# Late weight loads on ScalarE's queue, the last normalisation on VectorE, and the result's check behind the last product

## The chip, the cores and the metric

The kernel runs on one core of a Trainium2 chip. The metric is the time of one execution on the device, in microseconds (us); lower is better. Executions of a kernel scatter by some tenths of a per cent (the kernel before: 757.29 to 760.46 us in 11 runs), so two kernels are compared by runs on the same chip in the same rounds. All comparisons below are of runs in the fast state (one experiment was run a single time and its state is unknown; only its trace is used). Each ratio is to the kernel before.

## The reference

Two independent attention problems, A and B, of the same shape, with the outputs side by side:

```python
B, Sq, D = 16, 64, 640
H, Sk, Dh = 32, 512, 128
def ref(x, k_cache, v_cache, wq, wo):
    q = (x @ wq).reshape(B, Sq, H, Dh).transpose(0, 2, 1, 3)
    scores = einsum("bhqd,bhkd->bhqk", q, k_cache) * Dh ** -0.5
    o = einsum("bhqk,bhkd->bhqd", softmax(scores), v_cache)
    return o.transpose(0, 2, 1, 3).reshape(B, Sq, H * Dh) @ wo
return concatenate([ref(A...), ref(B...)], axis=-1)
```

All inputs are bf16. The K and V caches make up nearly all of the bytes, and each is read once.

## The kernel before

The work is cut into 128 **packs** of two batches and four heads. A planner gives every operation of every pack an engine and a time stamp in units of a pack (`AT`), sorts each engine's operations by it and derives the semaphore waits. Of one pack, in order: load K and V (LDK, LDV), query product and its copy (QP, QE), transposes of K on VectorE (KT), scores (S), exponentials with row sums (EX), reciprocals (RC), normalisation (NM), transposes of the probabilities on TensorE (TR) and their copies (TE), product with V (PV), its copy to SBUF (OE) and a zero fill of the PSUM bank (ZO), output product with wo (OP), and every fourth pack a sum (OS).

The stamps, the wo loads, the normalisation and the check, before the change:

```python
AT = dict(..., EX=(0.21, 0.32, 0.43, 0.54), RC=(0.53, 0.75), NM=(0.56, 0.69, 0.82, 0.95), TR=1.2,
          TE=(1.26, 1.39), PV=1.75, OE=(2.0, 2.06), ZO=2.11, OP=2.31, OS=2.53, ST=3.374, ...)
# ... wo: 16 loads of 640 KB, four at the start of each phase of 32 packs, in SyncE's list of loads
op = add("sp", "LDWO", w, n0 + AT["OP"] - 0.8 * NJ, [], [("wo", j)])
loads.append((n0 - NJ + AT["OP"] + 0.2 if ph else n0 - 1.9, 4, op))
# ... normalisation: four instructions per pack on GpSimd
add("pool", "NM", h, n + AT["NM"][i], [("p", h % cfg.NP), ("recip", n % cfg.NR, i // 3)], [("pn", i)])
# ... the check, once, beside the last pack
add("dve", "FL1", 0, N - 1 + AT["RC"][1] + 0.002, [("rs", h) for h in range(4 * N)], [("good",)])
add("pe",  "FLM", 0, N - 1 + AT["TR"] + 0.002, [("good",)], [("SB", 0)])
add("dve", "FLC", 0, N - 1 + AT["TE"][1] + 0.002, [], [("SB", 0), ("flag",)])
```

The **check** is there because the exponentials are taken without subtracting a maximum. FL1 tests on VectorE that every row sum lies within bounds, FLM adds the 128 answers up with a one-column matmul, and FLC writes the number as a flag. At its end every engine reads the flag and, if it is not 128, runs a second, general program:

```python
def run(e, eng):
    run_program(e, eng, 0)
    e.wait_ge(sems[0][("s_flc",)], 1)
    with e.register("flag_" + eng) as r:
        e.reg_load(r, flag[0:1, 0:1])
        with e.If_ne(r, 128):
            ...            # the general program, not taken with these inputs
    if eng == "act":
        all_done(e, 0, ("d_out",))
```

## Time and profile before

| | before |
|---|---|
| time, median of 3 runs (lowest to highest) | 757.39 us (756.77 to 757.5) |
| span in the trace | 756.0 us |
| waits of ScalarE's oT copy for wo | 18.6 us in B, 1.2 us in A |
| last exponential of the last pack ends | 742.64 us |
| from the last pack's first reciprocal to the start of the sum | 742.19 to 751.01 us |
| from the start of the sum to the end | 4.96 us |

The loads of wo pass through SyncE's queue, behind K and V. From the page's part on queues (packets, megabytes, share of the span of 16 DMA engines) and its part on issues (size of each, median us from issue to landing), of the kernel before:

```profile
q1 hardware_dynamic: 97456, 292.06, 98.8%
q10 hardware_dynamic: 2304, 2.62, 1.0%
...
wo_sb<-in_B_wo_dram SPq DMA_DIRECT2D x8, 640.0 KB, 13.3
```

q1 is SyncE's queue, q10 ScalarE's. The prediction shows the DMA row at its limit from the second slice to the last but two, and the serial tail.

### The profile page before, as it was taken

How to read it: one execution, taken by the hardware profiler on the slowest of the kernel's cores; microseconds unless marked ns; L12 is line 12 of the kernel's file. 1: busy time of each engine (PE TensorE's matmuls, PEld its weight loads, DVE VectorE, ACT ScalarE, POOL GpSimd, SP SyncE). 2: the span in 40 equal slices, each digit the busy share in tenths (PEclk: the TensorE clock that was granted, in tenths of full speed). 3: DMA queues.
4: the chain of work that ended last, by engine and by line, in shares of the span. 5: the costliest groups of instructions: out<-in, count | busy, mean ns of one | idle time of the engine just before them, and what ended most of it. 6: DMA issues, size and time to landing. Idle time of an engine off the chain costs nothing.

```text
span 756.0 us, 57362 instructions
## 1 busy us (share of the span) xinstructions
PE 685.2 (91%) x26518; PEld 530.0 (70%) x26518; DVE 533.2 (71%) x814; ACT 518.5 (69%) x1559; POOL 406.7 (54%) x584
## 2 busy tenths in 40 slices
PE   3669999999999989999988899999998899999995
PEld 2447777777777767777766677677776677777774
DVE  7436777777777777687766677777777577777772
ACT  2437787777777677767765777777766577777773
POOL 5434545555874554645684445446477265555542
PEclk9979999999999999999999999999999899999999
DMA  8999999999999999999999999999999999999980
GB/s 309 394 398 405 406 407 407 405 405 406 403 395 406 406 408 406 407 407 408 408 399 395 406 407 408 405 405 405 406 406 397 394 408 407 407 408 407 406 326 20
DMA packets 99805, 295.14 MB, mean 390 GB/s; under 512 B 9264, under 2 KB 24112, under 8 KB 99760
## 3 DMA queue, kind: packets, MB, share of 16 engines
q1 hardware_dynamic: 97456, 292.06, 98.8%
q10 hardware_dynamic: 2304, 2.62, 1.0%
q14 instruction: 35, 0.29, 0.1%
q8 instruction: 10, 0.16, 0.1%
HBM read 292.03 MB, written 2.62 MB: 390 GB/s over the span
## 4 chain that ended last, share of the span: by engine, by line
PE 40%; SPq 20%; DMA 17%; POOL 9%; DVE 8%; issue 4%; ACT 1%; POOLq 0%; DVEq 0%; ACTq 0%
PE ps L723 10%; PE ps L703 9%; POOL pn_sb L668 9%; PE ps L595 8%; SPq L544 8%; PE ps L618 7%; SPq L555 6%; PE ps L679 6%; DMA kn_ring<-in_B_k_cache_dram 6%; DMA kn_ring<-in_A_k_cache_dram 5%; SPq L557 4%; DMA wo_sb<-in_B_wo_dram 3%; DVE pT_sb L689 3%; DMA v_ring<-in_B_v_cache_dram 2%; DVE kt_ring L608 1%
## 5 line engine op out<-in xcount | busy, mean ns | idle before, releaser
L668 POOL TENSOR_SCALAR pn_sb<-p_ring,recip 128x512 bf16<-128x512 bf16 x512 | 344.5, 692 | 327.3 <-DVE recip L652 327.3
L608 DVE STREAM_TRANSPOSE kt_ring<-kn_ring 128x1024 f32<-128x1024 f32 x256 | 309.8, 1229 | 68.9 <-DMA kn_ring<-in_B_k_cache_dram 40.1
L639 ACT ACTIVATE p_ring<-ps 128x512 bf16<-128x512 f32 x512 | 298.3, 598 | 28.8 <-PE ps L618 20.2
L689 DVE COPY pT_sb<-ps 128x1024 bf16<-128x1024 bf16 x258 | 165.2, 682 | 113.4 <-PE ps L679 112.7
L723 PE MATMUL ps<-wo_sb,oT_sb 128*128 128x320 bf16 x1040 | 169.7, 307 | 6.9 <-issue 5.9
L595 PE MATMUL ps<-xT_ring,wqp_sb 128*128 128x128 bf16 x2560 | 166.9, 221 | 5.8 <-POOL xT_ring L584 5.6
L703 PE MATMUL ps<-pT_sb,v_ring 32*128 32x64 bf16 (+1 forms) x14528 | 155.5, 192 | 14.4 <-issue 6.4
L595 PEld LDWEIGHTS ps<-xT_ring,wqp_sb 128*128 128x128 bf16 x2560 | 158.5, 114 | 13.0 <-issue 5.8
L703 PEld LDWEIGHTS ps<-pT_sb,v_ring 32*128 32x128 bf16 (+1 forms) x14528 | 141.1, 92 | 27.7 <-issue 9.9
L711 ACT ACTIVATE oT_sb<-ps 128x256 bf16<-128x256 f32 x260 | 85.6, 381 | 107.1 <-PE ps L703 87.3
L618 PE MATMUL ps<-kt_ring,qs_ring 32*64 32x512 bf16 x4096 | 146.8, 397 | 0.0
L601 ACT ACTIVATE qs_ring<-ps 128x512 bf16<-128x512 f32 x128 | 76.5, 597 | 91.4 <-PE ps L595 91.2
L679 PEld LDWEIGHTS ps<-ident,pn_sb 64*128 64x128 bf16 x4128 | 71.1, 95 | 95.1 <-ACT ps L715 61.9
L723 PEld LDWEIGHTS ps<-wo_sb,oT_sb 128*128 128x128 bf16 x1040 | 92.9, 99 | 46.2 <-issue 6.3
L679 PE MATMUL ps<-ident,pn_sb 64*128 64x64 bf16 x4128 | 84.4, 192 | 34.4 <-POOL pn_sb L668 18.7
L639 ACT ACTIVATION_READ_ACCUMULATOR p_ring<-ps 128x1 f32 x512 | 106.6, 208 | 0.0
L618 PEld LDWEIGHTS ps<-kt_ring,qs_ring 32*64 32x64 bf16 x4096 | 55.5, 104 | 31.5 <-issue 0.9
L652 DVE RECIPROCAL recip<-rowsum 128x3 f32<-128x3 f32 (+1 forms) x256 | 37.3, 161 | 28.9 <-ACT p_ring L639 25.4
L715 ACT ACTIVATE ps<-zeros 128x256 f32<-128x256 bf16 x130 | 51.5, 396 | 0.0
L567 POOL COPY wqp_sb<-ws_sb 128x1280 bf16<-128x1280 bf16 x32 | 39.2, 1254 | 7.5 <-DMA ws_sb<-in_A_wq_dram 7.5
L584 POOL COPY xT_ring<-xs_sb 128x640 bf16<-128x640 bf16 x32 | 22.9, 716 | 3.1 <-PE ps L595 3.1
L574 PE MATMUL ps<-ident,xn_ring 128*128 128x128 bf16 x165 | 14.9, 222 | 4.2 <-DMA xn_ring<-in_A_x_dram 3.6
(25 smaller groups left out, 65.2 us busy)
## 6 DMA issues: line engine op xcount, KB each, us to landing
kn_ring<-in_A_k_cache_dram SPq DMA_DIRECT2D x128, 512.0 KB, 13.5
v_ring<-in_A_v_cache_dram SPq DMA_DIRECT2D x128, 512.0 KB, 12.1
kn_ring<-in_B_k_cache_dram SPq DMA_DIRECT2D x128, 512.0 KB, 14.5
v_ring<-in_B_v_cache_dram SPq DMA_DIRECT2D x128, 512.0 KB, 12.1
wo_sb<-in_A_wo_dram SPq DMA_DIRECT2D x8, 640.0 KB, 13.1
ws_sb<-in_B_wq_dram SPq DMA_DIRECT2D x10, 512.0 KB, 15.5
wo_sb<-in_B_wo_dram SPq DMA_DIRECT2D x8, 640.0 KB, 13.3
ws_sb<-in_A_wq_dram SPq DMA_DIRECT2D x4, 640.0 KB, 10.0
```

Of the source, the lines that this page charges most:

```text
L544: ins = e.dma_start(kn_ring[:, n % NK, b, :], src)
L595: last = e.matmul(ps[:, 1, f * 128:(f + 1) * 128], w[:, kt, f, :], xT_ring[:, xs, kt, :], start=(kt == 0), stop=(kt == KT - 1))
L601: ins = e.activation(qs_ring[:, op.idx % NQ].rearrange("p f b q -> p (f b q)"), ps[:, 1, :], ACTF.Copy, scale=scale)
L608: ins = e.transpose(dst, kn_ring[:, n % NK, b, :].bitcast(F32))
L618: last = e.matmul(ps[64 * b:64 * b + 64, i, :], qs_ring[rows, n % NQ, f, b, :], kt_ring[rows, n % NKT, b, :, f // 2, :, f % 2], start=(f = ...
L639: ins = e.activation(dst, src, ACTF.Exp, scale=1.0, accum_out=rowsum[:, h:h + 1])
L668: ins = e.tensor_scalar(dst, src, recip[:, h // 4 % NR, i:i + 1], 1.0, ALU.mult, ALU.mult)
L679: last = e.transpose(pt_bank(b)[:, 64 * c:64 * c + 64], pn_sb[rows, c, :], ident[rows, rows], tile_position=(64 * b, 0))
L689: ins = e.tensor_copy(pT_sb[:, b].rearrange("p t q -> p (t q)"), pt_bank(b))
L703: last = e.matmul(ps[:, 4 + i, 64 * b:64 * b + 64], v_ring[rows, n % NV, b, c, :], pT_sb[rows, b, c, :], start=(t == 0 and i < 2), stop=(t ...
L711: ins = e.activation(oT_sb[:, 2 * a:2 * a + 2, :], o_ps[:, 2 * a:2 * a + 2, :], ACTF.Copy)
L723: last = e.matmul(out_ps[:, s, :], oT_sb[:, i, :], wo_sb[:, 4 * j + i, s * NH0:(s + 1) * NH0], start=(j == 0 and i == 0), stop=(j == NJ - ...
```

## The change

Three parts. **wo**: the twelve wo loads of the later phases go from SyncE's queue to ScalarE's, so that they don't stand behind K and V. **Normalisation**: the last pack's four normalisations, which nothing covers, go from GpSimd to VectorE. **Check**: its reduces, matmul and flag move behind the last output product, out of the way of the last pack.

```diff
-  NM=(0.56, 0.69, 0.82, 0.95), TR=1.2,
+  NM=(0.56, 0.69, 0.82, 0.95), NMZ=(0.54, 0.55, 0.56, 0.76), TR=1.2,
-  OS=2.53, ST=3.374,
+  OS=2.53, LDWO=2.6, ST=3.374,
 ...
-            op = add("sp", "LDWO", w, n0 + AT["OP"] - 0.8 * NJ, [], [("wo", j)])
-            loads.append((n0 - NJ + AT["OP"] + 0.2 if ph else n0 - 1.9, 4, op))
+            if ph:
+                add("act", "LDWO", w, n0 - NJ + AT["LDWO"], [], [("wo", j)])
+            else:
+                loads.append((n0 - 1.9, 4, add("sp", "LDWO", w, n0 + AT["OP"] - 0.8 * NJ, [], [("wo", j)])))
 ...
-            add("pool", "NM", h, n + AT["NM"][i], ...)
+            add("pool" if n < N - 1 else "dve", "NM", h, n + (AT["NM"] if n < N - 1 else AT["NMZ"])[i], ...)
 ...
-        add("dve", "FL1", 0, N - 1 + AT["RC"][1] + 0.002, ...)
-        add("pe", "FLM", 0, N - 1 + AT["TR"] + 0.002, ...)
-        add("dve", "FLC", 0, N - 1 + AT["TE"][1] + 0.002, ...)
+        add("dve", "FL1", 0, N - 1 + AT["TE"][1] + 0.002, ...)
+        add("pe", "FLM", 0, N - 1 + AT["OP"] + 0.002, ...)
+        add("dve", "FLC", 0, N - 1 + AT["OS"] + 0.002, ...)
 ... (the rest gives operations of one kind on two engines their own semaphores)
```

More of the change, by code (lines that the diff above doesn't have):

```diff
@@ L31 @@
     AT = dict(XT=-2.485, XE=-2.28, XC=-0.9, QP=-0.45, QE=-0.24, KT=(-1.24, -1.0), S=0,
-              EX=(0.21, 0.32, 0.43, 0.54), RC=(0.53, 0.75), NM=(0.56, 0.69, 0.82, 0.95), TR=1.2,
-              TE=(1.26, 1.39), PV=1.75, OE=(2.0, 2.06), ZO=2.11, OP=2.31, OS=2.53, ST=3.374, WP0=-1.75, WP1=-1.6)
+              EX=(0.21, 0.32, 0.43, 0.54), RC=(0.53, 0.75), NM=(0.56, 0.69, 0.82, 0.95), NMZ=(0.54, 0.55, 0.56, 0.76), TR=1.2,
+              TE=(1.26, 1.39), PV=1.75, OE=(2.0, 2.06), ZO=2.11, OP=2.31, OS=2.53, LDWO=2.6, ST=3.374, WP0=-1.75, WP1=-1.6)
 class Op:
@@ L153, in build_plan @@
                 [("SB", i), ("p", h % cfg.NP), ("rs", h)])
-            add("pool", "NM", h, n + AT["NM"][i], [("p", h % cfg.NP), ("recip", n % cfg.NR, i // 3)], [("pn", i)])
+            add("pool" if n < N - 1 else "dve", "NM", h, n + (AT["NM"] if n < N - 1 else AT["NMZ"])[i], [("p", h % cfg.NP), ("recip", n % cfg.NR, i // 3)], [("pn", i)])
         for a in range(2):
@@ L158, in build_plan @@
     if not general:
-        add("dve", "FL1", 0, N - 1 + AT["RC"][1] + 0.002, [("rs", h) for h in range(4 * N)], [("good",)])
-        add("pe", "FLM", 0, N - 1 + AT["TR"] + 0.002, [("good",)], [("SB", 0)])
-        add("dve", "FLC", 0, N - 1 + AT["TE"][1] + 0.002, [], [("SB", 0), ("flag",)])
+        add("dve", "FL1", 0, N - 1 + AT["TE"][1] + 0.002, [("rs", h) for h in range(4 * N)], [("good",)])
+        add("pe", "FLM", 0, N - 1 + AT["OP"] + 0.002, [("good",)], [("SB", 0)])
+        add("dve", "FLC", 0, N - 1 + AT["OS"] + 0.002, [], [("SB", 0), ("flag",)])
     progs = {e: sorted((o for o in ops if o.eng == e), key=lambda o: o.ts) for e in ENGINES if e != "sp"}
@@ L217, in for_pe @@
         if d.kind == "NM":
-            return d.idx % 4 == 3
+            return d.idx % 4 == 3 and d.eng == "pool"
         if d.kind == "OS" and d.idx == N // NJ - 1:
@@ L226, in stand_in @@
                 return at[("QE", max(0, NJ * d.idx - 2))]
-            if d.kind == "NM":
+            if d.kind == "NM" and d.eng == "pool":
                 return at[("NM", d.idx | 3)]
@@ L265, in sem_key @@
             return ("d_out",)
-        return ("q_" + op.eng,) if for_pe(op) else ("s_" + op.kind.lower(),)
+        return ("q_" + op.eng,) if for_pe(op) else ("s_" + op.kind.lower() + "_" + op.eng,)
     for eng in ENGINES:
@@ L821, in run @@
             run_program(e, eng, 0)
-            e.wait_ge(sems[0][("s_flc",)], 1)
+            e.wait_ge(sems[0][("s_flc_dve",)], 1)
             with e.register("flag_" + eng) as r:
```

## The prediction

> **What bounds the kernel now.** I read the page first (parts 2 and 5), then the list of waits, then the windows by stage, then each K load's landing against the transpose that uses it, then the timeline of the last 17 us. The work is 128 packs (two batches, four heads each), in four phases of 32 packs; between phases a new quarter of wq and wo is loaded.
>
> ```profile
> span 756.0 us, 57362 instructions
> ...
> PE   3669999999999989999988899999998899999995
> ...
> DMA  8999999999999999999999999999999999999980
> GB/s 309 394 398 405 406 407 407 405 405 406 403 395 406 406 408 406 407 407 408 408 399 395 406 407 408 405 405 405 406 406 397 394 408 407 407 408 407 406 326 20
> ```
>
> The row DMA is full from the second slice until the loads run out near 735 us, at about 407 GB/s, and it sags to 394 to 399 only near 220, 400 and 590 us, where wq and wo are loaded. TensorE is nearly full too. So two limits lie side by side, and I have to find out which one holds where. The list of waits, cut to the stage around the last phase change (560 to 610 us), and the view of kn_ring from 605 to 735 us tell:
>
> ```profile
> ACT oT_sb L711 <- DMA wo_sb<-in_B_wo_dram: 8.6, 4, 3.3
> ...
> DVE kt_ring L608 <- DMA kn_ring<-in_B_k_cache_dram: 2.5, 5, 1.0
> ```
>
> ```profile
> L608 DVE STREAM_TRANSPOSE kt_ring<-kn_ring x50: 1200/1214/1227, 605.1 to 733.2; 128x1024 f32<-128x1024 f32 x50
> ```
>
> The second view lists nothing that these transposes waited for. Per pack, from the landing records: packs 8 to 35 find their K landed 4 to 8 us before the transpose (compute-bound). From pack 39 to pack 102 (236 to 598 us) the transpose starts the moment K lands, slack 0.0 (except 0.2 to 0.3 us at pack 99): the DMA sets the pace. From pack 103 (605 us) to the end K lies ready 0.3 to 1.4 us early, 0.6 at pack 127: compute sets the pace, just behind the DMA. What pushed compute behind is the wo wait: the lag from K's landing to the end of that pack's last exponential is 7.4 to 8.7 us while the DMA leads (most packs about 8.1), grows to 11.9 at pack 99 with the four waits for wo of 570 to 600 us, and is 10.05 at pack 127. It cannot be won back, because afterwards compute needs 21.15 us for four packs and K arrives every 5.30 us (21.2 for four).
>
> The end is a serial tail after the last K and V:
>
> ```profile
> 742.19 0.18 DVE L652 RECIPROCAL recip<-rowsum 128x3 f32<-128x3 f32 x1
> ...
> 742.46 2.69 POOL L668 TENSOR_SCALAR pn_sb<-p_ring,recip 128x512 bf16<-128x512 bf16 x4 [2.61 <-DVE recip L652]
> ...
> 744.07 0.40 ACT L715 ACTIVATE ps<-zeros 128x256 f32<-128x256 bf16 x1
> ...
> 745.30 0.73 PE L679 MATMUL ps<-ident,pn_sb 64*128 64x64 bf16 x32 [1.85 <-POOL pn_sb L668]
> 745.96 0.16 PE L759 MATMUL ps<-good 128*1 128x1 bf16 x1
> 746.05 1.26 PE L723 MATMUL ps<-wo_sb,oT_sb 128*128 128x320 bf16 x8
> 746.07 1.29 DVE L689 COPY pT_sb<-ps 128x1024 bf16<-128x1024 bf16 x2 [1.51 <-PE ps L679]
> 747.27 0.14 DVE L763 CAST flag<-ps 1x1 int32<-1x1 f32 x1
> 747.50 1.11 PE L703 MATMUL ps<-pT_sb,v_ring 64*128 64x64 bf16 x64 [0.19 <-DVE pT_sb L689]
> ...
> 751.01 0.82 DVE L736 TENSOR_TENSOR out_sb<-acc,ps 128x640 bf16<-128x640 f32 x1 [3.60 <-PE ps L723]
> 751.86 0.34 ACTq L742 DMA_DIRECT2D out_dram<-out_sb  x1
> ```
>
> TensorE idles 1.85 us for GpSimd's four normalisations. The check's reduces sit in VectorE's idle time, and its product holds TensorE for 0.09 us.
>
> [...] output stores on ScalarE's queue land in 5.5 to 6.3 us while SyncE's K loads take 13 to 17, so a second queue passes the backlog, but the total stays near 407 GB/s. [...] So a wo load on its own row shares bandwidth instead of standing behind SyncE's backlog. [...] every engine reads the flag and jumps over the general program, and then stands for 2.8 to 3.9 us (VectorE's branch ends at 752.05, its next record is 755.71; TensorE's own branch record is 3.84 us long, from 750.21 to 754.05), with instruction-queue packets of 8 and 16 KB in between.
>
> **The change part by part.**
>
> **wo on ScalarE's queue.** Twelve loads of 640 KB leave SyncE's list. In the new order each sits after the last exponential of pack n-2 and before the next query copy, and waits for the output product of pack n-4. That product ends about 0.8 us before those exponentials do (741.94 against 742.73), so ScalarE should not stall; issuing costs about 0.35 us (as the stores do), in the 0.35 to 0.98 us that ScalarE idles before the query copy anyway. Issue for pack 96 moves from 563.75 to about 559.5 (end of pack 94's exponentials), and landing takes an estimated 11 us (5.7 us for the 160 KB store, plus 24 more packets per DMA engine, each alternating with a 4 KB one at 58 + 162 ns: 5.3 us). So wo is there near 571, before the 577 us at which the oT copy first asks for it. All waits for wo (18.6 us for B, 1.2 for A) should go.
> What of it reaches the end? The first two phase changes lie before the DMA-led stretch, or in it: K slack is 0.0 through packs 64 to 71, though 10 us of wo waits stand there. The bytes are the same, so these return nothing. Only the last change counts, and only down to the DMA's floor. I walked the packs 98 to 127 forward: each ends at the later of its K landing plus 8.1 us and the previous pack plus its compute period (5.09, 5.08, 5.48, 5.50 in turn). Pack 127 then ends at 741.5 instead of 742.6: **1.1 us** (1.8 with a floor of 7.4, 0.5 with 8.7).
>
> **Normalisation on VectorE.** [...] successive ones overlap by about 0.08, as the two copies do (1.29 us for 2 x 682 ns). Reciprocal ends 742.37; [...] GpSimd ended at 745.15, and TensorE began 0.12 later, so the transposes start near 743.64, **1.65 us** earlier. Then a new wait: the output product of pack 126 needs ScalarE's zero fill, which ends at 744.47. The transposes end at 744.30, so it starts near 744.52 and ends at 745.78, just when the copies of VectorE end (745.70). The gain of 1.65 survives to the sum (749.36) and the store.
>
> **The check behind the last product.** It frees 0.09 us between transposes and output product, counted above. But all five engines read the flag before they may finish. Before, it stood at 747.4, and VectorE read it 0.39 us after its sum began. Now VectorE does the sum (0.82), the conversion to the flag (0.06 more after overlap), waits about 0.03, reads (0.54), branches (0.11) and fetches (3.66): from 749.36 that makes 754.58, against 749.36 + 4.70 = 754.06 without the move, so **0.5 us lost**. TensorE: flag at 750.24, read 0.5, branch 3.85, so 754.65, again later than the store path (ScalarE 755.57 - 1.65 = 753.9). So the tail is worth 1.65 - 0.55 = **1.1 us**.
>
> Sum: 1.1 + 1.1 = 2.2 us; 757.4 - 2.2 = 755.2. I shade it to 755.0 because K's landings may come a little earlier when SyncE no longer stops for wo (0.7 us of waits in that stage).
>
> **The rivals.** (a) **The wo waits all count**: 18.6 + 1.2 us, giving 738. For it: they are real idle time of ScalarE and TensorE. Against it: the DMA row is full all through, and K slack is zero around most of them. (b) **The transfer is hidden anyway**, because the DMA re-paces the last phase, or because wo in ScalarE's row delays K by the same 1.6 us each: only the tail is won, 756.3. For: K slack at pack 127 is only 0.6 us. (c) **The flag read becomes the end**: five fetches start within half a microsecond of each other and queue up, and the tail gains nothing: 756.3, or 757.4 together with (b). For: the 3.84 us branch. Against: fetches already overlap near 752 us. [...] (e) Mixed rows of 1280 B and 4 KB packets change the DMA rate: 1% over the stretch from 236 to 598 us would be 3.6 us either way.
>
> **Range and chances.** Best case: 1.8 from wo, 1.65 from the tail, a little rate: 753. Worst likely case: (b) with (c) or (d), 757. So 753.0 to 756.8 at 8 in 10. A 2% change is 15 us; only (a) comes near, and saturation speaks against it: faster 0.01, same 0.98, slower 0.01.
>
> **What would show it.** Right: no wait of the oT copy for wo; wo landing in about 11 us; K slack 0.0 in many packs after 103 and a lag near 8.5 at pack 127; [...] transposes of the last pack about 1.6 us sooner after the reciprocal; VectorE's or TensorE's branch, not the store, closing the span. Wrong: a K landing of pack 127 that moved by more than 1 us either way, waits of ScalarE before the query copy that grew, or the store still last.

The sum came to 2.2 us, 1.1 from wo and 1.1 from the tail (1.65 less 0.55), and so to 755.2, shaded to 755.0. Cut too are premises on queues and branches that no trace had shown, and rival (d), a slower normalisation on VectorE, which the range still names.

In the trace of the kernel before, ScalarE's output stores (128 packets of 1280 B, 57 ns each in the mean) landed in 6.0 us (median; 3.4 to 6.6), K in 15.3 (13.0 to 16.7, from 605 to 735 us). While a store's packets ran, between 241 and 719 us, 122 to 174 packets of SyncE's queue started, most of them of 4096 B at 164 ns: about one to one, which is what the estimate of 11 us takes for wo. Behind the branch on the flag, SyncE stood for 2.82 us, GpSimd for 3.10, VectorE for 3.66 and ScalarE for 2.60 (less than the 2.8 of the prediction); TensorE's branch took 3.84.

## More of the kernel before

`run_program` is a straight stretch, a loop over most of the packs, and a straight stretch for the last packs.

## The result

| | before | after |
|---|---|---|
| time, median of 4 runs | 757.08 us (756.76 to 757.5) | 758.62 us (758.03 to 759.57) |
| span in the trace | 755.97 us | 757.40 us |

The ratio is 1.0021, with a 95% interval of 1.0004 to 1.0039: the change made the kernel no faster, and in these rounds a little slower. A ratio here is the mean time of one kernel's fast runs over that of the other's fast runs of the same rounds, so it isn't quite the ratio of the medians beside it. A repeat (below) gave 1.0001 with an interval that holds 1, so a loss is not certain; the gain that was predicted is absent in both.

### The profile after

The page of the kernel after, span and the rows of the slices that answer to those of before:

```profile
span 757.4 us, 57362 instructions
...
PE   4579999999999989999978999899997999999995
...
DMA  8999999999999999999999999999999999999970
GB/s 309 394 399 405 406 406 407 406 405 407 400 395 409 407 408 406 407 407 407 406 394 401 406 407 407 406 405 405 406 403 395 406 408 407 402 409 406 407 294 16
...
q10 hardware_dynamic: 8640, 10.49, 3.8%
...
wo_sb<-in_B_wo_dram ACTq DMA_DIRECT2D x8, 640.0 KB, 10.9
```

The loads moved (q10 from 2.62 to 10.49 MB) and land in 10.9 us in place of 13.3. The DMA row is as full as before, and the rate is the same 407 GB/s.

The list of waits of the kernel after, in the stage around the last phase change (560 to 620 us; waiter, released by, us, times, longest), and the view of kn_ring from 605 to 735 us:

```profile
DVE kt_ring L610 <- DMA kn_ring<-in_B_k_cache_dram: 16.4, 14, 3.9
...
PEld ps L705 <- DMA v_ring<-in_B_v_cache_dram: 5.6, 5, 1.8
PE ps L705 <- DMA v_ring<-in_B_v_cache_dram: 4.8, 4, 1.6
```

```profile
L610 DVE STREAM_TRANSPOSE kt_ring<-kn_ring x50: 1204/1245/1248, 604.7 to 732.8; 128x1024 f32<-128x1024 f32 x50
...
  DMA kn_ring<-in_B_k_cache_dram: 6.9, 17
```

No line of the stage names wo any more. In its place VectorE waits 16.4 us for K (2.5 us before) and TensorE for V. The wo loads pass SyncE's queue, but at a full rate each of them pushes K and V back: the K of pack 99 lands at 583.3 us in place of 577.0. And the transposes of the last phase, which never waited for K before, now do so 17 times: the DMA sets the pace to the end.

The tail of the kernel after, from its timeline (start, busy us, engine, line and operation, out<-in, count, and in brackets the idle time before it and what ended that):

```profile
741.52 0.18 DVE L654 RECIPROCAL recip<-rowsum 128x3 f32<-128x3 f32 x1
741.73 0.88 DVE L670 TENSOR_SCALAR pn_sb<-p_ring,recip 128x512 bf16<-128x512 bf16 x3
...
742.72 0.35 DVE L670 TENSOR_SCALAR pn_sb<-p_ring,recip 128x512 bf16<-128x512 bf16 x1
742.84 0.66 ACT L713 ACTIVATE oT_sb<-ps 128x256 bf16<-128x256 f32 x2 [0.77 <-PE ps L705]
...
743.55 0.55 PE L681 MATMUL ps<-ident,pn_sb 64*128 64x64 bf16 x25 [0.79 <-ACT oT_sb L713]
745.32 0.29 PE L681 MATMUL ps<-ident,pn_sb 64*128 64x64 bf16 x7 [1.22 <-issue]
...
747.28 1.89 PE L705 MATMUL ps<-pT_sb,v_ring 64*128 64x64 bf16 x64
...
751.57 0.82 DVE L738 TENSOR_TENSOR out_sb<-acc,ps 128x640 bf16<-128x640 f32 x1 [3.00 <-PE ps L725]
752.31 0.14 DVE L765 CAST flag<-ps 1x1 int32<-1x1 f32 x1
752.42 0.34 ACTq L744 DMA_DIRECT2D out_dram<-out_sb  x1
```

VectorE's normalisation is done at 743.07, 1.55 us after the start of the first reciprocal; GpSimd needed 2.96. But the transposes are released by ScalarE's copy of the pack before (`<-ACT oT_sb`), then stop for 1.22 us between the 25th and the 26th with `<-issue`: TensorE waited there for nothing that the profile shows. And the product with V (64 matmuls) took 1.89 us, where it took 1.11 before. The windows view of that stage (window, length, busy us and counts of PE, PEld, DVE, ACT and POOL, granted clock, DMA share, GB/s), before and then after:

```profile
745.00:750.00 5.00, 3.48 (x108) 2.69 (x109) 1.34 (x3) 0.94 (x3) 0.15 (x1) 1.00 0.03 7
```

```profile
745.00:750.00 5.00, 3.84 (x79) 2.74 (x79) 2.85 (x7) 0.79 (x3) 0.00 (x0) 0.66 0.01 3
```

TensorE's granted clock was 0.66 in the mean: the records have it at 0.5 from 746.1 to 749.5 us, one window of 3.41 us.

The account between the two traces (us), by three points of the tail:

| stretch | before | after | difference |
|---|---|---|---|
| start to the last pack's first reciprocal | 742.19 | 741.52 | -0.67 |
| reciprocal to the start of the sum | 8.82 | 10.05 | +1.23 |
| sum to the end | 4.96 | 5.83 | +0.87 |
| span | 755.97 | 757.40 | +1.43 |

### The profile page after: what moved, and what is told of

The parts are those of the page before. It is cut to its first block, busy times and chain, and to the rows that moved or that the text cites. A ratio compares the mean times of both kernels' runs of the same rounds, so it can differ in the third digit from the quotient of the medians.

```text
span 757.4 us, 57362 instructions
## 1 busy us (share of the span) xinstructions
PE 682.2 (90%) x26518; PEld 528.0 (70%) x26518; DVE 536.7 (71%) x818; ACT 519.6 (69%) x1559; POOL 404.6 (53%) x580
## 3 DMA queue, kind: packets, MB, share of 16 engines
q10 hardware_dynamic: 8640, 10.49, 3.8%
HBM read 292.03 MB, written 2.62 MB: 389 GB/s over the span
## 4 chain that ended last, share of the span: by engine, by line
PE 33%; SPq 26%; DMA 19%; POOL 9%; DVE 8%; issue 5%; ACT 0%; POOLq 0%; DVEq 0%; ACTq 0%
SPq L546 12%; POOL pn_sb L670 8%; SPq L557 8%; PE ps L705 8%; PE ps L725 8%; PE ps L597 7%; DMA kn_ring<-in_B_k_cache_dram 6%; PE ps L620 6%; DMA kn_ring<-in_A_k_cache_dram 5%; PE ps L681 5%; SPq L559 5%; DMA v_ring<-in_B_v_cache_dram 5%; DVE pT_sb L691 3%; DMA v_ring<-in_A_v_cache_dram 3%; DVE kt_ring L610 1%
## 5 line engine op out<-in xcount | busy, mean ns | idle before, releaser
L610 DVE STREAM_TRANSPOSE kt_ring<-kn_ring 128x1024 f32<-128x1024 f32 x256 | 313.6, 1236 | 105.8 <-DMA kn_ring<-in_B_k_cache_dram 70.3
L725 PE MATMUL ps<-wo_sb,oT_sb 128*128 128x320 bf16 x1040 | 166.6, 303 | 5.9 <-issue 4.8
L654 DVE RECIPROCAL recip<-rowsum 128x3 f32<-128x3 f32 (+1 forms) x256 | 36.1, 158 | 24.5 <-ACT p_ring L641 21.2
## 6 DMA issues: line engine op xcount, KB each, us to landing
wo_sb<-in_B_wo_dram ACTq DMA_DIRECT2D x8, 640.0 KB, 10.9
ws_sb<-in_A_wq_dram SPq DMA_DIRECT2D x4, 640.0 KB, 10.1
```

Source lines behind the costliest of these rows:

```text
L610: ins = e.transpose(dst, kn_ring[:, n % NK, b, :].bitcast(F32))
L725: last = e.matmul(out_ps[:, s, :], oT_sb[:, i, :], wo_sb[:, 4 * j + i, s * NH0:(s + 1) * NH0], start=(j == 0 and i == 0), stop=(j == NJ - ...
```

## The experiments

**The theories.** T1, for the stop: the instructions behind TensorE's loop had not been fetched when TensorE got to them; the earlier start of the transposes only exposes it. Rival: a wait that the profile misses, tied to VectorE as the new producer. T2, for the clock: the tail's thin matmul work halves the granted clock now and then, whatever the kernel. Rival: the change causes it. T3, for the end: the late flag costs about 1 us. T4, for wo: the gain is real but small. Rival: K's landing takes all of it.

### The three parts alone

`e1_wo_only` is the kernel after, with normalisation and check as before:

```diff
-  add("pool" if n < N - 1 else "dve", "NM", ...)
+  add("pool", "NM", h, n + AT["NM"][i], ...)
-  FL1 at TE[1] + 0.002, FLM at OP + 0.002, FLC at OS + 0.002
+  FL1 at RC[1] + 0.002, FLM at TR + 0.002, FLC at TE[1] + 0.002
```

> Only the wo loads move to ScalarE's queue; the normalisation and the check are as before. Theory (a floor by the DMA): no wait for wo, K slack 0.0 in the last phase, the last exponential of pack 127 about 0.7 us sooner (742.0 against 742.6), the tail from there as before, so 0.7 us faster than before, no more. Rival (the second queue costs DMA rate, and the tail is innocent): K of pack 127 lands later and the time is 1 us or more above before. Rival (wo waits all count): several us faster.

Measured: 758.3 us (757.32 to 758.84, 5 runs), ratio 0.9991 [0.9976, 1.0006]. In its trace the last pack's first reciprocal starts 0.39 us sooner than in the trace of before. The interval of the time holds both the expected 0.7 us and nothing.

`e2_norm_only` is the kernel before with VectorE normalising the last pack:

```diff
-  add("pool", "NM", h, n + AT["NM"][i], ...)
+  add("pool" if n < N - 1 else "dve", "NM", h, n + (AT["NM"] if n < N - 1 else AT["NMZ"])[i], ...)   # NMZ last: 0.751
```

> Only the last pack's normalisation goes to VectorE; the check keeps its place, so its reduces now follow the normalisation on VectorE and its product stands before the output product of pack 126. Theory: the last transposes start about 1.1 us sooner after the last reciprocal (not 1.65: they also wait for ScalarE's copy of pack 126), but TensorE then stops for 1 to 1.4 us without any semaphore between the 25th and the 26th matmul of those 32, because its next instruction page has not come; the time is within 0.5 us of before, or 0.5 to 1.5 us slower where the clock is halved afterwards. Rival (no fetch stall): 1 us faster.

Measured: 756.83 us (756.12 to 760.6, 7 runs), ratio 0.997 [0.9955, 0.9984]. The same kernel again, on another chip, as `e14_norm_only_again`:

> The run with the normalisation alone, a second time, because its timed rounds were 1 us faster than before while its profile (with the clock halved through the tail) was 3 us slower. If the stop behind the 25th transposing matmul is there in every execution, it stays within 0.3 us of before where the clock is full; if the stop comes and goes, its profile shows a shorter one and the rounds are again 1 us faster.

Measured: 758.1 us (757.56 to 759.03), ratio 1.0004 [0.9989, 1.0019]. The two intervals don't meet, so this part alone is **inconclusive** in time. The traces say why it swings: both have the stop behind the 25th transpose, 1.32 us idle in the first and 0.93 us in the second, and the first has the clock at half from 745.4 us to the end, the second at full. From reciprocal to sum they take 11.94 and 8.78 us.

`e3_check_only` is the kernel before with the check moved:

```diff
-  FL1 at RC[1] + 0.002, FLM at TR + 0.002, FLC at TE[1] + 0.002
+  FL1 at TE[1] + 0.002, FLM at OP + 0.002, FLC at OS + 0.002
```

> Only the check moves behind the last product. Theory: the sum starts at most 0.1 us sooner, the flag is read 0.5 us later after it, five instruction fetches start together: 0.5 to 0.9 us slower than before. Rival (the store is the end and hides it): within 0.1 us of before.

Measured: 760.13 us (758.09 to 761.3), ratio 1.0016 [1.0000, 1.0033]. From the sum to the end it takes 5.83 us, exactly as in the kernel after and 0.87 more than before. T3 holds as far as one part alone can show it.

### Moving TensorE's instructions in memory

If the stop is a page of instructions that is not there yet, it must move when instructions are put in front of it. `e4_pad20` is the kernel after, with 20 increments of an unused semaphore at the start of TensorE's program:

```diff
+            if eng == "pe" and p == 0:
+                for _ in range(20):
+                    e.sem_inc(s_pad, 1)
```

> The changed kernel with 20 semaphore increments put in front of TensorE's program, where it waits for its first load. A test of the instruction-page theory: a matmul is two instructions, so the stop in the last pack's transposes should move from behind the 25th matmul to behind the 15th, 1.2 to 1.5 us long. Rival (the stop is a wait for data or a semaphore, or the clock): it stays behind the 25th, or vanishes.

Measured, in one look (758.86 us): the stop is there, elsewhere. The timeline of its transposes:

```profile
744.04 0.40 PE L681 MATMUL ps<-ident,pn_sb 64*128 64x64 bf16 x15 [0.79 <-ACT oT_sb L713]
745.68 0.43 PE L681 MATMUL ps<-ident,pn_sb 64*128 64x64 bf16 x17 [1.23 <-issue]
```

It stands behind the 15th transpose in place of the 25th. Each of these matmuls is two instructions, a weight load and the product (the page of the kernel after counts 26518 of each), so ten of them are the 20 instructions. The rival of T1 would have left it where it was. In the trace a 16 KB packet of the instruction queue runs at that time (742.55 to 743.90 us in the kernel after, 743.23 to 744.39 here), 2.1 to 2.2 us after TensorE left its loop, and the stop ends 1.3 to 1.4 us after the packet does. Before, the same packet ran from 743.28 to 744.24, when TensorE was waiting for GpSimd anyway until 745.30.

This run also had the clock at full in its tail. So its 9.08 us from reciprocal to sum, against 10.05 of the kernel after, give an estimate of what the halved window costs: 0.97 us. Two other runs agree: e3 above and e12 below do the tail up to the sum as the kernel before does, and with a halved window took 9.81 and 9.77 us against its 8.82.

`e5_pad226` has 226 increments, to put the boundary outside the transposes; that 226 would do so was the author's estimate, not read from a trace. `e7_mid_check_pad226` is the same with the check's matmul just ahead of the last output product and the flag ahead of the sum:

```diff
-                for _ in range(20):
+                for _ in range(226):
```
```diff
-  FLM at OP + 0.002, FLC at OS + 0.002
+  FLM at OP - 0.002, FLC at OS - 0.002      # e7 only
```

> The changed kernel with 226 semaphore increments at the front of TensorE's program, so that the page border leaves the last transposes [...]. Theory: no stop inside the 32 transposes; they end 2.7 us after the last long reciprocal's start and not 3.9; the end is 1 to 1.4 us sooner than the same kernel without the padding, if the clock is full in both. Rival (the stop comes of tracing or of something else): no gain in the timed rounds.

> As the padded one, and the check's product stands just before the last output product (where TensorE waits for ScalarE anyway) and the flag is written before the sum. Theory: the sum is read out and stored at the same time as in the padded kernel, but the flag is read some 0.4 us after the sum's start and not 0.9, and the engines' fetches no longer start together: 0.5 to 1.1 us faster than the padded kernel, so 1.5 to 2 us faster than before. Rival (the check costs nothing): equal to the padded kernel.

Measured: 777.31 us (776.82 to 777.68), ratio 1.0255 [1.0234, 1.0276], and 776.54 us (775.55 to 776.8), ratio 1.0242 [1.0221, 1.0263]. As a kernel this was a miss, by a cost that I had overlooked. The list of waits of the first:

```profile
PE ps L576 <- issue: 36.1, 1, 36.1
```

The 226 increments fill most of these 36.1 us, about 0.15 us each: in the kernel after, the first matmul starts at 3.49 us. About 20 us of it reach the end. The tail answers the question all the same. The transposes run through without a stop, the last one starting 2.49 us after the reciprocal in place of 3.90, and the sum starts at 7.66 in place of 10.05. Of this, 0.97 is the halved window; against e4, at full clock too, the missing stop is worth 1.42. The second tells the check's cost, with all else equal: 0.77 us less in time, and 4.82 in place of 6.25 us from sum to end, although all engines still read the flag.

### The better place for the check, and the kernel after again

`e9_mid_check` is the kernel after with this place of the check alone, `e8_after_again` the kernel after unchanged:

```diff
-  FLM at OP + 0.002, FLC at OS + 0.002
+  FLM at OP - 0.002, FLC at OS - 0.002      # e9 only
```

> The changed kernel with the check moved as in the last one, without padding: the stop in the transposes stays behind the 25th matmul (1.4 us), the end is 0.5 to 1.1 us sooner than the changed kernel, about equal to before.

> The changed kernel itself, for a comparison on this chip: 0.5 to 2 us slower than before, the stop behind the 25th transposing matmul in its profile, and a sixth to a half of its runs with the clock halved in the tail, about 1 us longer each.

Measured: 757.5 us (756.97 to 758.11), ratio 0.9993 [0.9975, 1.0012], against 758.06 us (757.41 to 759.32), ratio 1.0001 [0.9982, 1.0020]. From sum to end: 4.78 against 5.91 us. Both traces have the stop (0.91 and 1.07 us idle) and a halved window in the tail.

### Without the stop, at no cost

112 one-column matmuls are 224 instructions too, and TensorE has time for them at its start, while the first loads are on their way (its own first matmul then starts at 4.55 us in place of 3.5). `e10_mid_check_mm112` is e9 with them; `e11_norm_mid_mm112` is e10 with the wo loads back on SyncE; `e12_before_mm112` is the kernel before with the matmuls alone.

```diff
+            if eng == "pe" and p == 0:
+                e.wait_ge(sems[0][("s_init2_pool",)], 1)
+                for _ in range(112):
+                    e.matmul(ps[0:1, 0, 0:1], ident[:, 0:1], ident[:, 0:1], start=True, stop=True)
```

> All three parts, the check's product just before the last output product, and 112 matmuls of one column at the front of TensorE's program in place of the slow semaphore increments (they should fit into the wait for the first x, so the start is not delayed). Theory: no stop in the last transposes (their last starts 2.5 us after the long reciprocal), the span ends 12.5 us after that reciprocal as in the padded runs, and the time is 1.5 to 2 us below before. Rival (padding itself costs or gains elsewhere): not below before.

> The same without the wo part (wo loads by SyncE as before). Theory: the tail is the same 12.5 us, and the long reciprocal stands 0.4 to 0.7 us later, so this is 0.4 to 0.7 us slower than the one with wo moved, and 1 to 1.5 us faster than before. Rival (moving wo costs DMA rate and gains nothing): equal or faster than with wo moved.

> The kernel before with the same 112 one-column matmuls. A control: its transposes start only after the page has come, so padding should do nothing, within 0.3 us of before.

| kernel | median us (range) | ratio to before, 95% |
|---|---|---|
| e10, all three parts | 756.07 (755.76 to 756.41) | 0.9974 [0.9960, 0.9989] |
| e11, without the wo part | 755.86 (755.51 to 756.69) | 0.9969 [0.9955, 0.9983] |
| e12, before with the matmuls | 758.77 (756.79 to 759.22) | 1.0007 [0.9991, 1.0022] |

The timeline of TensorE in e10:

```profile
743.49 0.64 PE L681 MATMUL ps<-ident,pn_sb 64*128 64x64 bf16 x32 [0.79 <-ACT oT_sb L713]
744.06 1.26 PE L725 MATMUL ps<-wo_sb,oT_sb 128*128 128x320 bf16 x8
745.73 1.11 PE L705 MATMUL ps<-pT_sb,v_ring 64*128 64x64 bf16 x64 [0.41 <-DVE pT_sb L691]
```

All 32 transposes run in 0.64 us, and the product with V is back at 1.11. The sum starts 7.79 us after the reciprocal, 1.03 sooner than before. So these kernels beat the kernel before by 0.3%, where the kernel after had not; and since e12 is no faster than before, it isn't the matmuls that win by themselves. T1 holds.

The 0.3% is about 2.0 to 2.4 us, twice what the shorter tail gives. The runs of the kernel before in this call spanned 754.6 to 755.5 us where their mean clock was 0.988 or more, and 755.7 to 757.5 where it was 0.984 or less; e10's five spanned 754.0 to 754.7. So about 1 us is the tail, and the rest fits fewer halved windows, of which more now; where they fall in runs without a profile is not recorded.

For T2: halved windows fell in the tail of e1, e2, e3, e8, e9 and e12 and of the kernel after, and not of before, e4, e5, e7, e10, e11 and e14, nor of the two of the next section. e12 computes the tail as before does, and e2 and e14 are one kernel that shows both. So the change does not cause it by itself.

The kept traces show what goes with it. In each of the sixteen, all changes of the clock on record lie on one grid of 3.41 us steps. I cut each trace into its steps from 60 to 752 us. At full clock, 43 steps were followed by a halved one, and TensorE was busy for at most 52% of each; 3157 were followed by a full one, and TensorE was busy for at least 44% of each. (The ends of matmuls are modelled, so the border is not sharper than this.) By the windows view, a step of e2 with the halved one behind it, then a step of e14 and one of e10 with full ones behind them:

```profile
741.97:745.38 3.41, 1.76 (x153) 1.56 (x153) 3.11 (x12) 1.64 (x7) 0.00 (x0) 1.00 0.02 5
745.38:748.79 3.41, 2.74 (x20) 1.44 (x22) 1.34 (x3) 0.00 (x0) 0.00 (x0) 0.50 0.00 0
...
744.37:747.78 3.41, 2.30 (x57) 1.58 (x59) 2.38 (x8) 0.18 (x1) 0.00 (x0) 1.00 0.00 0
...
744.27:747.68 3.41, 2.32 (x73) 1.68 (x71) 2.90 (x8) 0.80 (x3) 0.00 (x0) 1.00 0.02 5
```

TensorE was busy for 1.76 us of e2's step; in e14 the grid lies otherwise over the same tail, and its step has 2.30. So in these traces it took both, an idle stretch and a grid that falls badly on it. Slid freely over the tail up to the sum, a stretch of 3.41 us is busy for as little as 37% in before and 41% in the kernel after, but never under 57% in the six traces without GpSimd's wait and without the stop (e5, e7, e10, e11 and the two of the next section). None of the six has a halved window before the sum: in the shorter tail no 3.41 us are as idle as the steps that came before a halved one, busy for at most 52%. T2 is right for the kernel before, and wrong in "whatever the kernel".

### What the wo part is worth

The pair of e10 and e11 differs in the wo part alone and shows nothing (756.07 and 755.86), although in most traces the last reciprocal is sooner with it. So the pair was run again, unchanged:

> The combined kernel again, unchanged, with the wo loads on ScalarE. If the earlier start of the tail that the traces show (the last pack's reciprocal starts 0.3 to 1.0 us sooner with the wo part than without) is real in the time, this kernel is 0.5 to 0.9 us below its partner without the wo part in the same rounds. If the wo part is worth nothing, the two lie within 0.3 us of each other, as in the round before (756.07 against 755.86).

> The same kernel with the wo loads back on SyncE, unchanged from the round before. Expected against the kernel before: ratio 0.9965 to 0.9985 again. Against its partner of this call: 0.5 to 0.9 us slower if the wo part is worth its share of the prediction, within 0.3 us if it is not.

Measured: with the wo part 756.02 us (755.37 to 756.3), ratio 0.9962 [0.9947, 0.9976]; without it 755.59 us (755.38 to 757.82), ratio 0.9965 [0.9948, 0.9981]. Twice the same answer: within these few runs the wo part is worth **nothing** that shows, and T4's gain is not borne out. Why the traces had shown a gain is told by the second trace of the kernel without it. The windows from 602 to 606 us, just after its last wait for wo, in e11 and then in e16, which are the same program:

```profile
602.00:606.00 4.00, 4.00 (x55) 3.35 (x55) 3.65 (x7) 1.66 (x7) 1.65 (x3) 0.57 1.03 411
```

```profile
602.00:606.00 4.00, 4.00 (x191) 3.32 (x189) 3.74 (x7) 2.70 (x10) 2.15 (x4) 1.00 1.03 410
```

TensorE had stood for 2.4 to 2.5 us while the oT copy waited for wo. In e11 the clock was then halved for one window, and TensorE started 55 matmuls in these 4 us; in e16 it was at full, and it started 191 (most of them the 128 small ones of the next product with V, which e11 reached only at 605.84). The grid tells the two apart: of the step before, TensorE was busy for 1.31 us in e11 (598.94 to 602.35) and for 1.64 in e16 (599.13 to 602.55). Both traces have all four waits for wo of that stage, 10.1 and 10.2 us together:

```profile
ACT oT_sb L711 <- DMA wo_sb<-in_B_wo_dram: 10.1, 4, 3.2
```

(This line is e11's.) From pack 90 to pack 101 the last exponentials of the two agree within 0.3 us; from pack 103 on e16 is 1.3 to 1.5 us ahead. The lag from K's landing to the last exponential at pack 127 is 10.01 us in e11, 8.84 in e16, 8.91 with the wo part in e15 and 9.18 in the kernel after. So what the wo part removes from the end is not the waits for wo but one slow window of TensorE that follows them where the grid falls badly. It pays for this with the last K, which lands at 732.5 to 733.6 us in the traces with it (the two slow kernels e5 and e7 aside) and at 732.55 to 732.70 in those without. In e16, without the slow window, VectorE waits for K in the last phase as often as in the kernel after (17 times, 7.2 us in all): the DMA sets the pace there too.

One thing stays open. Six of the seven traces without the wo part have the slow window near 601 us, yet the timed runs show no loss from it. The unprofiled runs of e11 have spans of 753.8 to 754.1 us against 755.0 of its profiled one, and those of e16 lie, but for one, within 0.6 us of its own. That fits runs without the slow window, but the time of a halved window is not recorded outside the profiles, so it is not shown.

## Why the prediction was wrong

The predicted 755.0 us (753.0 to 756.8) missed the measured 758.62, and the gain that it forecast did not come. The class (within 2%) was right. By its steps:

- **Saturation, and rival (a).** Right. The DMA row and the 407 GB/s are unchanged, and taking away 18.6 us of waits for wo brought no several microseconds.
- **"All waits for wo ... should go", landing in an estimated 11 us.** Right: none left in that stage, 10.9 us. Rival (b) was right as well, though: the bytes then delay K and V, and the wait moved to K.
- **1.1 us from wo.** 0.66 us in the trace (the last exponential of pack 127 ends at 741.98 in place of 742.64), none in the timed pairs. The floor of 8.1 us, a mean over another stage, was too low for this pack. With the DMA setting the pace, the last four packs lagged 8.2 to 8.8 us in e16 and 8.5 to 9.2 in the kernel after, pack 127 the most in both. And the prediction's "What pushed compute behind is the wo wait" does not stand: e16 has the same waits and 8.84 us at the end. By comparison, 1.2 us of the 10.05 in before go with the halved clock behind the last wait, which the prediction did not look at.
- **Normalisation.** 0.35 us each in the trace, so the fourth ended 1.55 us after the reciprocal's start, in place of the 1.33 that the predicted start of the transposes implies (743.64, less 0.12, less 742.19). A small miss, which nothing waited for.
- **"so the transposes start near 743.64, 1.65 us earlier".** The first step that failed: 1.08 us. They also wait for ScalarE's oT copy of pack 126. The trace of before has it from 743.52 to 744.18, 1 us before GpSimd was done, so it showed no wait there; but transposes at 743.64 would have had to start in the middle of it. The prediction looked for the new wait one step later, at the zero fill.
- **"The gain of 1.65 survives to the sum".** The step that turned the sign. In the kernel after, the sum starts 1.23 us later after the reciprocal, not 1.65 sooner. The runs show what took its place: a stop for instructions, which with the smaller start gain makes +0.26 in all at a full clock (e4: 9.08 against 8.82; e14, with a stop of 0.93 in place of 1.23, has 8.78), and one halved window, +0.97. Take the stop away (e10, e11) and the 1.08 us do survive: 1.03 at the sum.
- **The check, 0.5 us lost.** The right mechanism, the size too small: 0.87 us in e3 and in the kernel after, about 1.1 in the mean of all traces (5.83 to 6.25 us from sum to end with the late flag, 4.71 to 5.08 with an early one), 0.77 us in the timed pair e5 and e7. The prediction used 3.66 us for VectorE's jump; with five engines jumping within 0.35 us it took 3.95 (753.13 to 757.08). That the flag and not the store ends the span was right: the store had landed at 754.27, 3.1 us before the end.

The range was too narrow because the prediction knew the instruction fetches only at the jump at the end, not behind the loop, and did not look at the tail's clock, which comes in two kinds that differ by 1 us. On the first, the traces show a 16 KB packet of the instruction queue and a stop that moves with the instruction count, from behind the 25th transpose to behind the 15th for 20 instructions (e4). The packet came as late before the change (743.28 to 744.24 us), where the wait for GpSimd, to 745.30, covered it; after the change it left TensorE idle for 0.9 to 1.3 us in six traces. In the kernel after, TensorE left the loop at 740.50 and the packet ran only from 742.55. On the second, the records show the clock at 0.5 for steps of 3.41 us, on a grid that keeps its place all through a trace, and e2 and e14 show how this gives one kernel both kinds: of the step before a halved one, TensorE was busy for at most 52%, be it for a wait of 2.4 us within busy code (e11, near 600 us) or for a thin tail.

## What to carry to other kernels

Before predicting that a serial tail gets shorter by what one engine saves, list everything that its consumer waits for and when each would be ready, and look in the trace for instruction-queue packets in that stretch: a wait may be hiding a fetch behind a loop's end. Here it hid one, and removing the wait won nothing (+0.26 us to the sum at a full clock, e4) until the boundary was moved (-1.03, e10). Where a flag must be read by every engine before the end, write it as early as its inputs allow, and not last (4.78 against 5.91 us from the sum to the end, e9 and e8). Count, too, how busy TensorE is in the thinnest 3.41 us of the tail: in these traces half the clock, and 1 us, was lost only where that was about half or less (at most 52%). And ask what a load that passes another pushes back: here, at 407 GB/s, the waits for wo went (8.6 us in the last phase change), and those for K grew from 2.5 to 16.4 us.

## Measured on the way

- Behind the branch over the general program, at the end, the engines of the kernel after stood for 3.12 us (SyncE) to 3.95 us (VectorE); TensorE's branch took 3.65. Before, it was 2.60 (ScalarE) to 3.84 us (TensorE).
- The bf16 tensor_scalar of 512 elements, written in eight blocks of 64, took 0.35 us on VectorE (the kernel after); on GpSimd the last pack's four took 2.69 us together (the kernel before).
- Instructions on TensorE that only increment a semaphore took about 0.15 us each, 226 in a row at the start of its program (e5), and made the kernel 20 us slower; 112 one-column matmuls near the same place added nothing that shows (e12: ratio 1.0007).
